# Attention and FFN kernel: the first FFN product of batches 3 to 6 with two block pairs as seven half products for eight

## The chip, the cores and the metric

The kernel runs on one core of a Trainium2 chip. The metric is device microseconds of one execution. The figure compared is the median over several runs.

## The reference

There are 8 batches, 8 heads of 64 columns, 512 local and 32 global positions. The local queries see the global keys and a band of 32 positions to each side; the global queries see everything. The result is the input of an FFN with a sigmoid gelu.

```python
s_g = scale * q_g @ concat(k_g, k_l).T          # global rows: no mask
out_g = softmax(s_g) @ concat(v_g, v_l)
s_ll = where(|i - j| <= 32, scale * q_l @ k_l.T, -1e9)
out_l = softmax(concat(scale * q_l @ k_g.T, s_ll)) @ concat(v_g, v_l)
x = concat(out_g, out_l) per batch, heads side by side   # 8 * 544 rows, 512 columns
h = x @ w_in                                     # 512 -> 2048, the first FFN product
out = (h * sigmoid(1.702 * h)) @ w_out           # 2048 -> 512, the second
```

## The kernel before

All work is laid out by hand: the order of the instructions in the program is the order on each engine's queue. Heads go in two groups of four, a `Quad` each: `a` is the first of a batch, `c` the second, `a2` the first of the batch after. The local rows of a batch are 512 tokens, held as `xL[i]` (model columns in four chunks of 128 on the partitions); the global rows of all batches gather in `xG` and are worked as a ninth batch at the end.

From batch 3 on the program alternates two stages.

**`h_some(i)`, the first FFN product of batch i.** The 2048 columns are 16 blocks of 128 (`fc`). A plain block (`h_step`) is four matmuls of 512 columns (line 617) into a PSUM bank `hp`, then a gelu on ScalarE (line 622) into `gT`. Blocks 2 and 3 are a block pair `g = 1`, worked by `HPair` in Winograd's form: seven products of half the columns and half the depth, two matmuls of 256 columns each (line 699), where eight would be needed. It takes weight sums made once, during batch 0 (`h_weight_sums`, line 660, kept in `early`), and sums of the input `xL` made on VectorE at the end of the stage before (`x_sums`, lines 673 and 674). The steps around the products are `m3` (copy on ScalarE), `z`, `zm`, `sub`, `add` on VectorE (lines 707, 710, 713, 716), and two gelus `inner` and `outer`. The pair's products lie in the two tiles of `spair()`, four PSUM banks. Batch 7 has a second `HPair` for `g = 4`. Between the blocks VectorE turns the keys and queries that the coming attention needs (`Tk`, `Tq`, lines 512 and 316), and `kcopy`, `qcopy` and `ext` copy parts of them and of the global keys and queries into place (lines 504, 507, 538 to 545). VectorE also makes `g_sums(i, lo, hi)`: four sums over block pairs lo to hi of `gT`, for the second product (lines 770 and 773). `k` is 0, 1, 2, 3, and the sum with `k = 2` is twice as long.

**`phase_o(i)`, the second product of batch i with the attention of batch i + 1.** The second product is Winograd too (`Pair`, line 800): `p0` and `p1` are two halves of the tokens, with `px` and `py` as banks. Between the products TensorE makes the scores (`S`, line 560) and the weighted values (`U` and `Gm`, together `UG`, lines 586 and 597). ScalarE takes the exponentials (`X`, line 571). `M` multiplies them with the band mask (line 576): on VectorE, but `a2.M(0)` on GpSimd. `R` makes the reciprocal of the row sums: a transpose `sT` (line 462), a reciprocal `rT` and a transpose back `rs`. `XL` multiplies the values with it into `xL`. `G` normalizes a quad's global rows and transposes them into `xG` (lines 476, 478, 479).

```python
exp_table()
a.UG()
c.S(0)
a.R()
g_sums(i, 7, 8, (0,))
a.XL(0)
g_sums(i, 7, 8, (1, 2))
a.XL(1)
g_sums(i, 7, 8, (3,))
p0.mm(3, 4, 1)
```

The matmul banks (`hp`, `ov`, `og`, `px`, `py`) rotate through four PSUM banks: `px` after `a.UG()` takes the bank of the first `ov`, which `R`'s `sT` frees, and `py` that of the second, which `XL(0)` frees. `loads_after` issues the loads of later batches from GpSimd's queue: nine for the values, one each for queries and keys.

Of the kernel before, what the change touches and what calls it, by code (L numbers as in the profile page):

```python
# [12 lines left out]
F32 = mybir.dt.float32  # L13
BF16 = mybir.dt.bfloat16
# [6 lines left out]
def kernel(  # L21
# [12 lines left out]
    nc = tc.nc  # L34

    B, H, Sl, D = q_l.shape
# [23 lines left out]
    att = ctx.enter_context(tc.tile_pool(name="att", bufs=2))  # L60
# [51 lines left out]
    def on_act(out_, in_):  # L112
        nc.scalar.activation(out_, in_, AF.Copy)  # L113
# [30 lines left out]
    early = ld.tile([128, 4, TB], F32, name="early", bufs=1)  # L144
# [131 lines left out]
    xG_by_row = xG.rearrange("p k (a s f) -> p k a s f", a=2, f=4)  # L276
# [3 lines left out]
    def pbank(name):  # L280
        return psP.tile([128, 512], F32, name=name, tag="p")
# [218 lines left out]
    class Wide(Quad):  # L500
# [100 lines left out]
        def UG(self):  # L601
            for unit in range(3):
                self.U(unit)
            self.Gm()

    gTs, ops = {}, {}
    HT = TB // 2
    HM = d_model // 2

    def width(i):  # L610
        return TB if i < B else B * Sg
# [23 lines left out]
    def exp_table():  # L635
        nc.scalar.activation(spot[:, 0:1], spot[:, 1:2], AF.Exp)

    def h_act(i, fc, hp):
        n = width(i)
        gelu(gTs[i][:, fc, :n], hp[:, :n])  # L640

    def h_step(i, fc):
        if fc == 0:
            gTs[i] = (moe.tile([128, FC, TB], BF16, name="gT") if i < B else
                      early.bitcast(BF16).rearrange("p a b -> p (a b)").rearrange("p (f t) -> p f t", f=FC))
        hp = pbank("hp")
        h_mm(i, fc, hp, range(NKC))
        h_act(i, fc, hp)

    w_h = {g: [w_in_c[:, g // 2, 2 * k : 2 * k + 2, g % 2, :, e] for e in range(2) for k in range(2)]  # L650
           for g in (1, 4)}
    w_s = early.bitcast(BF16).rearrange("p a b -> p (a b)")[:, : 5 * 2 * 256].rearrange(
        "p (k u c m) -> p k u c m", k=5, u=2, c=2)
    wh = {g: [w_s[:, k, u] for k in range(5)] for u, g in enumerate(w_h)}

    def h_weight_sums(g):
        w11, w12, w21, w22 = w_h[g]
        for t, x, y, op in zip(wh[g], (w11, w21, w11, w21, w12), (w22, w22, w12, w11, w22),
                               (ALU.add, ALU.add, ALU.add, ALU.subtract, ALU.subtract)):
            nc.vector.tensor_tensor(t, x, y, op)  # L660
# [93 lines left out]
    def g_sums(i, lo, hi, which=(0, 1, 2, 3)):  # L754
        n = width(i)
        if i not in sums:
            if i < B:
                sums[i] = [moe.tile([128, FC // 2, w * HT], BF16, name="gs%d" % k)
                           for k, w in enumerate((1, 1, 2, 1))]
            else:  # L760
                room = [ld.tile([128, 2, 16 * D], BF16, name=x).rearrange("p a b -> p (a b)")
                        for x in ("rk", "rq", "rk")]
                sums[i] = [x.rearrange("p (g t) -> p g t", g=FC // 2)
                           for x in (room[0][:, :1024], room[0][:, 1024:], room[1], room[2][:, :1024])]
        a11, a12, a21, a22 = parts_of(i)
        t = gTs[i].rearrange("p (g e) t -> p g e t", e=2)
        g = slice(lo, hi)
        for k in which:
            if k == 2:
                nc.vector.tensor_tensor(sums[i][2][:, g, :n], t[:, g, 0, :n], t[:, g, 1, :n], ALU.add)  # L770
            else:
                x, y, op = {0: (a11, a22, ALU.add), 1: (a21, a11, ALU.subtract), 3: (a12, a22, ALU.subtract)}[k]
                nc.vector.tensor_tensor(sums[i][k][:, g, : n // 2], x[:, g], y[:, g], op)  # L773
# [75 lines left out]
    a, c = Quad(0), Quad(1)  # L849
# [81 lines left out]
    for fc in range(4, FC):  # L931
        h_step(0, fc)
        if fc == 4:
            h_weight_sums(1)
        if fc == 12:
            h_weight_sums(4)

    def osteps(i, *sts):
# [4 lines left out]
    a, c = nq[1]  # L943
# [71 lines left out]
    a, c = nq[2]  # L1015
# [22 lines left out]
    def loads_after(i):  # L1038
        if i + 2 < B:
            load_v(i + 2)  # L1040
        if i == 1:
            load_g(8, NQ)
        if i + 3 < B:
            load(i + 3)
# [49 lines left out]
    def phase_o(i):  # L1094
        b = i + 1
        a, c = nq[b]
        a2, c2 = quads_of(b + 1)
        p0, p1 = Pair(i, 0), Pair(i, 1)
        exp_table()
        a.UG()  # L1100
        c.S(0)
# [7 lines that stand above are left out]
        c.X(0)  # L1109
        p0.m3()  # L1110
        p0.z()
        a.G()
        c.M(0)
        c.S(1)
        c.X(1)
        p0.mm(6)
        p0.zm()
        c.M(1)
        p0.mm(5, 2)
        p0.sub()  # L1120
        p0.evict()
        p0.mm(7)
        p0.add()
        p0.store()
        if a2:
            c.UG()
            c.R()
            a2.S(0)
            a2.X(0)
            a2.M(0, nc.gpsimd)  # L1130
            loads_after(i + 1)
        else:
            pt = spair()
            c.U(0, bank(pt, 0))
            c.U(1, bank(pt, 2))
            c.U(2, bank(pt, 3))
            c.Gm(bank(pt, 1))
            c.R()
        c.XL(0)
        if a2:  # L1140
            c.XL(1)
            c.G()
        p1.mm(3, 4)
        p1.m3()
        p1.z()
        if not a2:
            c.XL(1)
            c.G()
        p1.mm(1, 6)
        p1.zm()  # L1150
        x_sums(i + 1)
        if a2:
            a2.S(1)
            a2.X(1)
        p1.mm(5, 2)
        p1.sub()
        p1.evict()
        gelu_table()
        p1.mm(7)
        p1.add()  # L1160
        if a2:
            a2.M(1)
        p1.store()

    def h_some(i):
        c = nq[i + 1][1] if i + 1 < B else None
        a2 = quads_of(i + 2)[0] if i + 2 < B else None
        pool = nc.gpsimd.tensor_copy
        gTs[i] = moe.tile([128, FC, TB], BF16, name="gT")
        hps = [pbank("hp"), pbank("hp")]  # L1170
        for fc in range(2):
            h_mm(i, fc, hps[fc], range(NKC))
        p = HPair(i, 1)
        p.mm(3, 4)
        p.m3()
        for fc in range(2):
            h_act(i, fc, hps[fc])
        if c:
            c.Tk(False)
            c.kcopy(pool)  # L1180
        p.z()
        p.mm(1, 6)
        p.zm()
        if c:
            c.Tq(False)
            c.qcopy(pool)
            c.ext((3,), pool)
        if a2:
            a2.Tk(False)
            a2.kcopy(pool)  # L1190
        h_step(i, 4)
        if c:
            c.ext((0,), on_act)
        h_step(i, 5)
        p.mm(5, 2)
        p.sub()
        p.inner()
        p.mm(7)
        p.add()
        h_step(i, 6)  # L1200
        p.outer()
        if a2:
            a2.Tq(False)
            transpose_g(2 * i + 4, 2 * i + 6)
            a2.qcopy(pool)
            a2.ext(copy=pool)
        if c:
            g_sums(i, 0, 2)
        h_step(i, 7)
        if c:  # L1210
            c.ext((1,), on_act)
            g_sums(i, 2, 4)
            for fc in range(8, 12):
                h_step(i, fc)
                if fc == 9:
                    c.ext((2,), on_act)
            g_sums(i, 4, 6)
            h_step(i, 12)
            h_step(i, 13)
            g_sums(i, 6, 7)  # L1220
            h_step(i, 14)
            h_step(i, 15)
            return
        p = HPair(i, 4)
        p.mm(3, 4)
        p.m3()
        g_sums(i, 0, 2, (0, 1))
        p.z()
        p.mm(1, 6)
        p.zm()  # L1230
        g_sums(i, 0, 2, (2,))
        h_step(i, 10)
        h_step(i, 11)
        p.mm(5, 2)
        p.sub()
        p.inner()
        p.mm(7)
        p.add()
        g_sums(i, 0, 2, (3,))
        h_step(i, 12)  # L1240
        p.outer()
        for k in range(3):
            for lo in (2, 4):
                g_sums(i, lo, lo + 2, (k,))
        h_step(i, 13)
        h_step(i, 14)
        h_step(i, 15)
        g_sums(i, 6, 8, (0, 1, 2))
        g_sums(i, 2, 4, (3,))
        g_sums(i, 4, 6, (3,))  # L1250
        g_sums(i, 6, 8, (3,))

    for i in range(1, B):
        if i > 2:
            h_some(i)
        elif i > 1:
            for fc in range(FC):
# [3 lines left out]
                if i + 1 < B:  # L1261
                    c = nq[i + 1][1]
# [6 lines left out]
                    if fc == 9 and i + 2 < B:  # L1269
                        a2 = quads_of(i + 2)[0]  # L1270
# [19 lines left out]
    for st in range(FC):  # L1290
        h_step(B, st)
        if st < len(todo):
            tt, k = todo[st]
            if k == 3:
                p = Pair(B - 1, tt, pair_banks(tt))
# [19 lines left out]
    p = Pair(B, 0, (x0, x1, y0, y1))  # L1315
# [53 lines left out]
```

## Time and profile before

| what | value |
|---|---|
| median of 3 runs | 285.36 us (285.32 to 285.5) |
| profiled execution, its own time | 285.7 us |
| its span | 284.0 us |
| TensorE busy | 277.0 us (98%) |
| VectorE busy | 228.9 us (81%) |
| ScalarE busy | 182.1 us (64%) |
| GpSimd busy | 107.1 us (38%) |
| granted TensorE clock | 1.0 throughout |

The profile shows one execution. Its span runs from the first to the last instruction; the execution's own time is 1.7 us longer. In the timeline, an instruction's row gives its start, its length, and in brackets the idle time of its engine before it with what ended that. Successive rows of one engine can overlap by a tenth or two, because an instruction starts while the one before it drains; so the time from start to start is what a row of instructions costs, and the length is what one of them takes until others may use its result. "PE s L699" and "PE s L617" are matmuls into the tiles of `spair()`.

### The profile page before, as it was taken

Reading aid. Unit: us, or ns where it says so; the run is one execution under the profiler, and the core shown is the slowest. Engines: PE = TensorE matmul, PEld = TensorE weight load, DVE = VectorE, ACT = ScalarE, POOL = GpSimd, SP = SyncE. Lnnn points to the kernel's source line nnn. Section 1 sums busy time; section 2 is a strip of 40 time slices with the busy share of each in tenths; the row PEclk is TensorE's granted clock in tenths of the full one; section 3 lists DMA queues with packets and bytes.
Section 4 is the critical chain, followed back from the end, with each engine's and each line's share of the span. In section 5 each row is a group of like instructions: output and inputs, shape, how many; then the busy total and the mean of one; then the engine's idle time right before and its main releaser. Section 6 shows DMA issues by size and latency. Waiting matters only on the chain.

```text
span 284.0 us, 9001 instructions
## 1 busy us (share of the span) xinstructions
PE 277.0 (98%) x3763; PEld 182.3 (64%) x3763; DVE 228.9 (81%) x518; ACT 182.1 (64%) x299; POOL 107.1 (38%) x172
## 2 busy tenths in 40 slices
PE   7899999999999999999999999999999999999994
PEld 6454445544554488746885588647875589558884
DVE  7584458986689899999989998999988898586452
ACT  4858757577778784688457873788459761873331
POOL 8993550765946001990079302960041000000001
PEclk9999999999999999999999999999999999999999
DMA  7999995899999801795039802980022003200223
GB/s 208 159 195 210 203 162 77 148 217 144 170 165 183 151 2 48 78 177 91 14 69 163 150 5 68 84 97 3 21 58 74 2 3 76 74 3 0 58 54 112
DMA packets 59352, 28.24 MB, mean 99 GB/s; under 512 B 47472, under 2 KB 49776, under 8 KB 59312
## 3 DMA queue, kind: packets, MB, share of 16 engines
q0 software_dynamic: 51760, 17.83, 56.2%
q1 hardware_dynamic: 7120, 9.18, 11.7%
q8 instruction: 29, 0.48, 0.7%
q10 hardware_dynamic: 432, 0.66, 0.7%
q14 instruction: 11, 0.09, 0.1%
HBM read 36.31 MB, written 8.91 MB: 159 GB/s over the span
## 4 chain that ended last, share of the span: by engine, by line
PE 86%; DVE 7%; DMA 2%; issue 1%; POOL 1%; ACT 1%; DVEq 0%; POOLq 0%; ACTq 0%
PE hp L617 31%; PE px L800 12%; PE op L731 10%; PE py L800 9%; PE x L800 6%; PE s L560 5%; PE ov L586 5%; PE s L699 3%; PE s L617 3%; DMA rq<-in_q_l_dram 2%; DVE gs L773 2%; DVE gs L770 1%; DVE xL L471 1%; DVE kT L512 1%; PE og L597 1%
## 5 line engine op out<-in xcount | busy, mean ns | idle before, releaser
L617 PE MATMUL hp<-xL,w_in_sb 128*128 128x512 bf16 x432 | 97.0, 379 | 0.2 <-DVE xL L471 0.2
L617 PEld LDWEIGHTS <-w_in_sb 128*128 128x128 bf16 x528 | 51.4, 98 | 51.8 <-issue 0.4
L622 ACT ACTIVATE gT<-hp 128x512 bf16<-128x512 f32 x108 | 62.7, 600 | 17.1 <-PE hp L617 16.6
L571 ACT ACTIVATE e<-s 128x1016 bf16<-128x1016 f32 (+1 forms) x56 | 53.3, 1003 | 25.7 <-PE s L560 25.7
L800 PEld LDWEIGHTS <-gs 128*128 128x128 bf16 x480 | 46.2, 98 | 6.6
L576 POOL TENSOR_TENSOR e<-e,mask 128x1760 bf16<-128x1760 bf16 x4 | 13.3, 3320 | 70.0 <-ACT e L571 70.0
L98 POOL DMA_DIRECT2D v<-in_v_l_dram x40 | 31.1, 780 | 13.6 <-PE og L597 3.8
L773 DVE TENSOR_TENSOR gs<-gT 128x512 bf16<-128x512 bf16 (+1 forms) x87 | 31.6, 398 | 3.3 <-ACT gT L622 3.3
L800 PE MATMUL py<-wsum,gs 128*128 128x256 bf16 x240 | 30.3, 273 | 0.0
L731 PE MATMUL op<-w_out_sb,gT 128*128 128x512 bf16 x128 | 29.5, 380 | 0.0
L576 DVE TENSOR_TENSOR e<-e,mask 128x1712 bf16<-128x1712 bf16 (+1 forms) x24 | 25.2, 1049 | 3.5 <-ACT e L571 3.5
L512 DVE STREAM_TRANSPOSE kT<-rk 128x512 f32<-128x512 f32 x14 | 14.5, 1037 | 12.6 <-DMA rk<-in_k_l_dram 12.6
L833 POOL DMA_DIRECT2D out_dram<-ob x2 | 1.2, 596 | 60.5 <-ACT ob L113 60.3
L731 PEld LDWEIGHTS <-gT 128*128 128x128 bf16 x128 | 11.8, 98 | 14.0
L800 PEld LDWEIGHTS <-gT 128*128 128x128 bf16 x192 | 18.0, 98 | 3.0
L800 PE MATMUL px<-w_out_sb,gT 128*128 128x256 bf16 x160 | 19.2, 273 | 0.1
L800 PE MATMUL px<-w_out_sb,gs 128*128 128x256 bf16 x160 | 19.1, 273 | 0.0
L471 DVE TENSOR_TENSOR xL<-ov,rs 128x512 bf16<-128x512 f32 x27 | 17.9, 686 | 1.0 <-PE ov L438 0.3
L113 ACT ACTIVATE ob<-px 128x512 f32<-128x512 f32 x10 | 6.0, 599 | 19.3 <-DVE zz L822 19.3
L770 DVE TENSOR_TENSOR gs<-gT 128x1024 bf16<-128x1024 bf16 (+1 forms) x29 | 17.2, 598 | 0.0
L560 PEld LDWEIGHTS <-kT 32*128 32x128 bf16 x672 | 12.5, 93 | 6.8 <-issue 5.7
L100 POOL DMA_DIRECT2D v<-in_v_g_dram x24 | 14.0, 585 | 2.2 <-DMA rq<-in_q_l_dram 1.7
(176 smaller groups left out, 429.3 us busy)
## 6 DMA issues: line engine op xcount, KB each, us to landing
out_dram<-ob SPq DMA_DIRECT2D x128, 64.0 KB, 2.7
rq<-in_q_l_dram POOLq DMA_DIRECT2D x5, 512.0 KB, 8.2
rk<-in_k_l_dram POOLq DMA_DIRECT2D x5, 512.0 KB, 10.0
v<-in_v_l_dram POOLq DMA_DIRECT2D x24, 96.0 KB, 4.8
w_in_sb<-in_moe_w_in_dram POOLq DMA_DIRECT2D x8, 256.0 KB, 6.9
w_out_sb<-in_moe_w_out_dram POOLq DMA_DIRECT2D x4, 512.0 KB, 10.1
rk<-in_k_l_dram POOLq DMA_DIRECT2D x5, 256.0 KB, 7.8
rq<-in_q_l_dram POOLq DMA_DIRECT2D x5, 256.0 KB, 7.2
```

Of the source, the lines that this page charges most:

```text
L98: nc.gpsimd.dma_start(out=vt[0:n, hs, c, :D], in_=vs[FIRST[c] : FIRST[c] + n, hs])
L471: nc.vector.tensor_mul(self.x[:, 2 * self.u + h, :], self.st[1 + h], self.st["rs"])
L512: nc.vector.transpose(flat[:, 0:Sl].rearrange("p (r t) -> p t r", t=16), loaded[self.b][0][:, self.u].bitcast(F32))
L560: nc.tensor.matmul(bank(self.ps, j)[:, at : at + n], lhsT=self.k[p, KEYS[c] : KEYS[c] + 128, e], rhs=qs[p, :, :, e], start=(e == 0), stop= ...
L571: nc.scalar.activation(self.E[rnd][:, 2 * i : 2 * i + 2, :n], self.ps[i][:, :, :n], AF.Exp, scale=scale)
L576: eng.tensor_mul(e, e, mask[:, rnd : rnd + 1, :n].to_broadcast([128, 4, n]))
L617: nc.tensor.matmul(hp[:, : width(i)], lhsT=w_in_c[:, fc // 4, kc, fc % 4 // 2, :, fc % 2], rhs=(xL[i] if i < B else xG)[:, kc, :], start=( ...
L622: nc.scalar.activation(out_, in_, AF.Gelu_apprx_sigmoid)
L731: nc.tensor.matmul(op, lhsT=gTs[i][:, fc, tci * 128 : tci * 128 + 128], rhs=w_out_sb[:, fc, :], start=(first and fc == 4 * f4), stop=(fc = ...
L770: nc.vector.tensor_tensor(sums[i][2][:, g, :n], t[:, g, 0, :n], t[:, g, 1, :n], ALU.add)
L773: nc.vector.tensor_tensor(sums[i][k][:, g, : n // 2], x[:, g], y[:, g], op)
L800: nc.tensor.matmul(out_, lhsT=lv[:, g, tt * 128 : tt * 128 + 128], rhs=rv[:, g, :], start=(g == 0 and k in ((1, 3, 4, 6) if self.apart els ...
```

## The change

In `h_some` of batches 3 to 6 a second block pair, `g = 2` (blocks 4 and 5), joins `g = 1` in one `HPair`, so each of its steps works on twice the columns. A third group of weight sums is made for it in batch 0. Around it:

- `c.Tq` and `a2.Tk` move ahead of the pair's `z`, and c's copies with them; the loads move from `phase_o` to behind these copies.
- `g_sums` runs in three sets (pair 0, pairs 1 to 3, pairs 4 to 6) instead of four.
- The mask product of `a2` in round 0 moves from GpSimd to VectorE, behind `p1.z()`; that of round 1 moves from VectorE to GpSimd, at the end of `phase_o`.
- `a2`'s copies move from GpSimd in `h_some` to ScalarE in `phase_o` (for i over 2).
- `G` of the two quads becomes one `GG`, on a copy that ScalarE makes of each quad's PSUM result (`keep_og`).

```diff
+    def keep_og(q, ogs):
+        on_act(ogs[:, q.u], q.st["og"][:, : D + 2])
+
+    def GG(b, ogs):
+        rg = att.tile([128, 2, 1], F32, name="rgg")
+        nc.vector.reciprocal(rg, ogs[:, :, D : D + 1])
+        xg = att.tile([128, 2, D], BF16, name="xgg")
+        nc.vector.tensor_mul(xg, ogs[:, :, :D], rg.to_broadcast([128, 2, D]))
+        for u in range(2):
+            nc.vector.transpose(xG_by_row[:, 2 * u : 2 * u + 2, b // 4, :, b % 4],
+                                xg[:, u].rearrange("p (d h) -> p h d", h=2))
...
-           for g in (1, 4)}
+           for g in (1, 2, 4)}
...
         if fc == 12:
+            h_weight_sums(2)
             h_weight_sums(4)
...
 def phase_o(i):
+        ogs = att.tile([128, 2, D + 2], F32, name="ogs", bufs=1)
+        late = a2 and i > 2
...
         p0.z()
-        a.G()
+        keep_og(a, ogs)
+        if late:
+            a2.kcopy(on_act)
+            a2.qcopy(on_act)
         c.M(0)
         c.S(1)
         c.X(1)
         p0.mm(6)
         p0.zm()
         c.M(1)
+        if late:
+            a2.ext(copy=on_act)
         p0.mm(5, 2)
...
             c.UG()
             c.R()
+            keep_og(c, ogs)
             a2.S(0)
             a2.X(0)
-            a2.M(0, nc.gpsimd)
-            loads_after(i + 1)
...
         if a2:
             c.XL(1)
-            c.G()
+            GG(b, ogs)
         p1.mm(3, 4)
         p1.m3()
         p1.z()
-        if not a2:
+        if a2:
+            a2.M(0)
+        else:
             c.XL(1)
-            c.G()
+            GG(b, ogs)
...
         if a2:
-            a2.M(1)
+            a2.M(1, nc.gpsimd)
         p1.store()
...
 def h_some(i):
-        p = HPair(i, 1)
+        gs = (1, 2) if c else (1,)
+        fcs = iter([fc for fc in range(2, 8) if fc // 2 not in gs])
+        p = HPair(i, *gs)
         p.mm(3, 4)
         p.m3()
         for fc in range(2):
             h_act(i, fc, hps[fc])
         if c:
             c.Tk(False)
             c.kcopy(pool)
+            c.Tq(False)
+            c.qcopy(pool)
+            c.ext((3,), pool)
+            loads_after(i)
+        if a2:
+            a2.Tk(False)
         p.z()
         p.mm(1, 6)
         p.zm()
         if c:
-            c.Tq(False)
-            c.qcopy(pool)
-            c.ext((3,), pool)
-        if a2:
-            a2.Tk(False)
-            a2.kcopy(pool)
-        h_step(i, 4)
+            g_sums(i, 0, 1)
+        h_step(i, next(fcs))
         if c:
             c.ext((0,), on_act)
-        h_step(i, 5)
+        h_step(i, next(fcs))
         p.mm(5, 2)
         p.sub()
         p.inner()
         p.mm(7)
         p.add()
-        h_step(i, 6)
-        p.outer()
         if a2:
             a2.Tq(False)
             transpose_g(2 * i + 4, 2 * i + 6)
-            a2.qcopy(pool)
-            a2.ext(copy=pool)
-        if c:
-            g_sums(i, 0, 2)
-        h_step(i, 7)
-        if c:
+        if not c:
+            h_step(i, next(fcs))
+            p.outer()
+            h_step(i, next(fcs))
+        else:
+            h_step(i, 8)
+            p.outer()
+            g_sums(i, 1, 4)
+            h_step(i, 9)
             c.ext((1,), on_act)
-            g_sums(i, 2, 4)
-            for fc in range(8, 12):
-                h_step(i, fc)
-                if fc == 9:
-                    c.ext((2,), on_act)
-            g_sums(i, 4, 6)
+            h_step(i, 10)
+            c.ext((2,), on_act)
+            h_step(i, 11)
             h_step(i, 12)
             h_step(i, 13)
-            g_sums(i, 6, 7)
+            g_sums(i, 4, 7)
             h_step(i, 14)
             h_step(i, 15)
             return
```

More of the change, by code (lines that the diff above doesn't have):

```diff
@@ L650 @@
     w_h = {g: [w_in_c[:, g // 2, 2 * k : 2 * k + 2, g % 2, :, e] for e in range(2) for k in range(2)]
-           for g in (1, 4)}
-    w_s = early.bitcast(BF16).rearrange("p a b -> p (a b)")[:, : 5 * 2 * 256].rearrange(
-        "p (k u c m) -> p k u c m", k=5, u=2, c=2)
+           for g in (1, 2, 4)}
+    w_s = early.bitcast(BF16).rearrange("p a b -> p (a b)")[:, : 5 * 3 * 256].rearrange(
+        "p (k u c m) -> p k u c m", k=5, u=3, c=2)
     wh = {g: [w_s[:, k, u] for k in range(5)] for u, g in enumerate(w_h)}
@@ L1138, in phase_o @@
             c.R()
+            keep_og(c, ogs)
         c.XL(0)
```

## The prediction

> **What bounds the kernel now.** I read the page's chain that ended last first, then the same chain in order of time, then each engine's timeline around one batch. All times are microseconds of the profiled execution.
>
> ```profile
> PE 86%; DVE 7%; DMA 2%; issue 1%; POOL 1%; ACT 1%; DVEq 0%; POOLq 0%; ACTq 0%
> ```
>
> TensorE carries the end nearly alone. The chain in time shows what each piece costs it (start, length):
>
> ```profile
> 163.78 0.64 DVE sT L462
> 164.46 1.91 PE px L800 x16
> 166.37 0.96 PE py L800 x8
> ...
> 180.35 1.73 PE hp L617 x8
> 182.08 0.87 PE s L699 x8
> 182.95 1.73 PE hp L617 x8
> 184.68 0.66 PE s L699 x6
> 185.34 8.63 PE hp L617 x40
> 193.97 1.20 PE ov L586 x59
> ```
>
> The last six lines are the first FFN product of batch 5, from 180.35 to 193.97, without a gap: a 512-column matmul takes 1.73/8 = 0.216, a half product of 256 columns 0.87/8 = 0.109. The first three lines are the one place in batches 3 to 6 where VectorE led: px waited for R's first transpose (sT). The windows of two `phase_o` stages, cut where TensorE starts `a.UG()`, price that:
>
> ```profile
> 162.39:180.35 17.96, 17.82 (x393) 15.24 (x394) 16.71 (x38) 10.85 (x14) 4.78 (x4) 1.00 0.14 34
> 193.97:211.66 17.69, 17.69 (x393) 15.19 (x394) 16.16 (x36) 10.74 (x14) 3.32 (x1) 1.00 0.13 33
> ```
>
> Columns: stage, length, then busy time (and instructions) of PE, PEld, DVE, ACT, POOL. With sT starting 1.32 after the stage's start (163.71) the stage lost 0.28; where it started 0.70 after (194.67) or 1.09 after (132.14, stage of 17.67), nothing. VectorE is busy 16.2 of 17.7 here and 13.3 of 13.6 in the first product, so what it does last before sT decides. Its rows, and those of the engines it waits for:
>
> ```profile
> 143.99 3.32 POOL L576 TENSOR_TENSOR e<-e,mask 128x1760 bf16<-128x1760 bf16 x1 [16.21 <-ACT e L571]
> 145.86 2.07 DVE L673 TENSOR_TENSOR sT<-xL 128x512 bf16<-128x512 bf16 x2
> 239.86 0.73 DVE L673 TENSOR_TENSOR sT<-xL 128x512 bf16<-128x512 bf16 x2
> ...
> 191.18 0.68 DVE L770 TENSOR_TENSOR gs<-gT 128x1024 bf16<-128x1024 bf16 x1
> 191.78 1.08 DVE L773 TENSOR_TENSOR gs<-gT 128x512 bf16<-128x512 bf16 x3
> ...
> 246.48 0.69 DVE L713 TENSOR_TENSOR ob<-ob,s 128x512 f32<-128x512 f32 x1 [0.91 <-PE s L699]
> ...
> 21.10 1.94 ACT L622 ACTIVATE gT<-s 128x1024 bf16<-128x1024 f32 x2 [3.52 <-PE s L617]
> 192.28 0.60 ACT L622 ACTIVATE gT<-hp 128x512 bf16<-128x512 f32 x1 [0.27 <-PE hp L617]
> ```
>
> Two x-sums take 2.07 while GpSimd runs its mask product and 0.73 (batch 7) without it. The last row is the gelu of block 13: it waits only for TensorE and ends at 192.88, 1.09 before the stage.
>
> **The change on TensorE.** Per batch 3 to 6, eight matmuls of 0.216 (1.73) become fourteen of 0.109 (1.53): -0.20, four times **-0.80**. The 0.098 weight load of each half product stays under its 0.109. [...]
>
> **Edits that I cost at nothing, with their cover.**
> - Weight sums of the third group: five more of 0.34 start-to-start, 1.7, behind 24.85; VectorE then idles 7.34 until the keys land at 32.19.
> - Masks: the product moved to VectorE is 1.06, the one moved off 1.04. The x-sums lose the contention (2.07 to 0.73). GpSimd's 3.32 now starts when X(1) ends, 0.8 before the first product, and has 14 until `a.UG()`. Behind it stand c's three copies (about 1.2, done at 3.9 into the product, needed at 15) and then the loads (nine of v, and in two batches q and k, up to 8): issued some 5.5 later, needed 20 later at the least.
> - Global outputs: two G of 0.68 start-to-start become one GG, about 0.9 (reciprocal 0.20, product 0.35, two transposes 0.17 each). One G leaves `p0`, where VectorE next waits for X(1) anyway; the other end grows 0.2. GG waits for `keep_og(c)`, ready at 10.5 of the stage, asked for at 12.6.
> - ScalarE's copies: `keep_og` is bounded by its copies of 0.29 (72 elements) and 0.37 (256); I take 0.26 each. kcopy and qcopy, by the same rows 0.33 and 0.5, stand ahead of c's X(1); m3 starts at 3.85 of the stage, so they end by 5.0, and X(1) starts at 5.27 today. Were that gone, the mask product, sub, evict and c.UG would follow late one for one. The four of `ext` (0.9) lie between 7.05 and the evict at 8.87.
> - Moving c.Tq and a2.Tk ahead of z: after x-sums without contention and no mask product behind `p1.add`, VectorE reaches c.Tk at 0.64 into the product instead of 2.36, z at 3.1; mm(5, 2), which overwrites what z reads, comes at 5.20. Without this cover z would cost up to 1.6.
>
> **The edit that costs: the tail of the first product.** Count from its start, with the stage beginning at 1.73 + 0.87 + 0.87 + 1.73 + 0.87 + 0.44 + 6.91 = 13.41.
> - sub follows mm(5, 2), at 6.10. On 512 elements it takes 0.68, on 256 0.41, so about 1.21 on 1024: 7.31. add: 7.41 to 8.63.
> - ScalarE is in order: inner (1024 elements, 0.92 start-to-start) from 7.34, gelu 8 at 8.26 (0.48), outer at 8.74 (0.95, source in SBUF), then gelus 9 to 12 (0.48 each) and two `ext` copies (0.21, 0.16): gelu 13 runs 11.98 to 12.58. Today's ends 1.09 before the stage; this one 0.83 before.
> - Sums of block pairs 1 to 3 wait for outer (9.79) and end at 12.1. Sums of pairs 4 to 6 wait for gelu 13. Start-to-start a sum is 0.20 on 256 elements, 0.34 on 512, 0.60 on 1024; so 0.47 on 768 and 0.87 on 1536, and the set is 3 x 0.47 + 0.87 = 2.28. Today only the last pair's set (0.94) needs gelu 13; the set of pairs 4 and 5 (1.61) can go before it.
> - sT so starts at 12.61 + 2.28 = 14.89, 1.48 into the stage, in all four batches. Queued behind it on VectorE are rT, rs and the product that frees py's bank; px waits for sT, py for that product.
>
> Price: at 1.32 the stage lost 0.28. One for one, 1.48 loses 0.44; by the transpose alone (px free at 1.13 at the latest by py's start of 3.79) 0.35. I take 0.39, the middle: four times **+1.56**. Batch 4's present 0.28 is contained in that: **-0.28**.
>
> **Sum.** -0.80 - 0.28 + 1.56 = +0.48 on the profiled execution's own 285.7 (span 284.0, 1.7 around it): 286.2. That run lies 0.3 above the median of 285.36; on the median it is **285.8**, +0.17%. About 0.2% (0.57) is what a measurement of this kernel can tell from no change.
>
> **The rivals.**
> - *The tail stays covered (faster).* If gelu 13 and the sums end 0.35 earlier, sT starts by 1.13 and nothing waits: -0.80 - 0.28, 284.3; half covered, 284.8. For it: in batch 6 VectorE waits 0.56 before sT, and its load falls by the contention. Against it: the 2.28 behind gelu 13 depend on no earlier slack. 0.18.
> - *The tail is longer (slower).* sub and add cost like two of 512 each (0.77 start-to-start, so 1.54 instead of 1.31). outer then starts at about 9.2 and everything behind it is 0.46 later: 0.85 a batch, +3.4 - 1.08, 287.7. It decides as soon as the loss exceeds 0.42 a batch, so a fifth of it is enough for 286.0 to 286.4. 0.38.
> - *The exchanged mask collides.* GpSimd's product made the first x-sum wait to its end (147.26). [...] In the new order the last x-sum starts at about 16.1 of the stage and the GpSimd product 0.84 later. If the x-sums come 0.84 later, the last one waits until 2.6 into the product; sub, add, three transposes and z follow, z ends at 7.7 where 5.2 was due: at least 2.5 a batch, 295. 0.05.
> - That the half products are not made is excluded by the built order: TensorE has 24 more matmuls.
>
> **How the numbers follow.** The forecast, 284.8 to 285.9, has 0.39. Chances: faster 0.18, same 0.39, slower 0.43 (0.38 and 0.05). The likeliest case is the sum, 285.8. The range reaches down past the half-covered tail to 284.5 and up to 287.0, which is 0.67 lost a batch, some two thirds of the way to the longer tail's full price; outside lie the fully covered tail, the end of the longer one, and the collision.
>
> **What would show it.** Right: in batches 3 to 6 gelu 13 ends about 0.8 before `phase_o`, the four sums on 768 and 1536 elements run from there without a gap, sT starts about 1.5 into the stage, and px follows it at once; the first product is 13.4 and the stages 18.0 to 18.1. Two x-sums at 0.73 show the exchange as costed. Wrong: stages of 17.7 (covered), TensorE waiting at mm(5, 2) (z late), x-sums near 2 or more, or X(1) waiting behind qcopy.

## The result and the profile after

The changed kernel takes 287.82 us by the median of 6 runs (286.86 to 288.5), the kernel before 285.36 (285.3 to 285.61): the ratio of the runs is 1.0078, 95% interval 1.0061 to 1.0095 (the two medians alone would give 1.0086). It is slower. The forecast was 285.8 in a range of 284.5 to 287.0; the result lies above it. The profiled execution is the fastest of the six, 286.86, with a span of 285.1.

The chain that ended last now has ScalarE in it, which the kernel before hadn't beyond 1%:

```profile
PE 79%; ACT 9%; DVE 8%; DMA 1%; issue 1%; SPq 0%; DVEq 0%
```

In order of time (start, length), from the last half products of batch 3's first FFN product into `phase_o(3)`:

```profile
122.02 0.89 PE s L711 x8
122.93 1.23 DVE ob L725
124.19 2.94 ACT gT L634 x4
127.34 0.49 ACT gT L634
127.98 1.47 ACT gT L634 x3
129.47 1.03 DVE gs L785 x2
130.50 0.87 DVE gs L782
131.36 0.47 DVE gs L785
131.83 0.64 DVE sT L462
132.51 1.91 PE px L812 x16
134.42 0.96 PE py L812 x8
135.59 0.49 issue
136.07 0.53 PE s L560 x13
```

Down to px this is the forecast's tail, step by step: mm(5, 2), sub, the gelus up to block 13, the four sums of pairs 4 to 6, sT. The last two lines are not in the forecast: TensorE stands for 0.49 in the middle of `c.S(1)`, waiting for nothing that the profile shows. The view of the waits, TensorE's rows, gives both (total, times, longest):

```profile
PE px L812 <- DVE sT L462: 1.3, 4, 0.3
PE s L560 <- issue: 0.5, 1, 0.5
```

The stages of batches 4 and 5, cut where `a.UG()` starts and where the next first product starts, answer to those of before (17.96 and 17.69):

```profile
162.47:180.63 18.16, 17.82 (x393) 15.25 (x394) 16.96 (x35) 12.86 (x23) 0.65 (x1) 1.00 0.37 75
194.04:212.20 18.16, 17.83 (x393) 15.24 (x394) 16.96 (x35) 12.85 (x23) 0.66 (x1) 1.00 0.14 33
```

Both lose 0.47 against an undisturbed 17.69; TensorE's busy time is that of the stalled stage before (17.82), 0.13 above the undisturbed one's 17.69. Counted from the first matmul of one `a.UG()` to that of the next, batch 4's stage and first product take 31.57 and batch 3's 32.24. So the gap in `c.S(1)` costs 0.67 there, more than the 0.49 that stands as idle time. And the rows that the forecast rested on:

```profile
114.18 0.74 DVE L685 TENSOR_TENSOR sT<-xL 128x512 bf16<-128x512 bf16 x2
129.47 1.03 DVE L785 TENSOR_TENSOR gs<-gT 128x768 bf16<-128x768 bf16 x2 [0.43 <-ACT gT L634]
...
199.79 1.89 ACT L571 ACTIVATE e<-s 128x992 bf16<-128x992 f32 x2 [0.36 <-PE s L560]
```

Two x-sums take 0.74, as costed. VectorE waits for gelu 13 before the last sums. c's X(1) waits for TensorE's scores, not for the copies put ahead of it.

### The profile page after: what moved, and what is told of

Same layout as the page of the kernel before. It is cut to its first block, busy times and chain, and to the rows that moved or that the text cites. A ratio compares the mean times of both kernels' runs of the same rounds, so it can differ in the third digit from the quotient of the medians.

```text
span 285.1 us, 9001 instructions
## 1 busy us (share of the span) xinstructions
PE 275.1 (96%) x3764; PEld 184.7 (65%) x3787; DVE 227.3 (80%) x497; ACT 188.7 (66%) x319; POOL 99.1 (35%) x154
## 4 chain that ended last, share of the span: by engine, by line
PE 79%; ACT 9%; DVE 8%; DMA 1%; issue 1%; SPq 0%; DVEq 0%
PE hp L629 22%; PE px L812 13%; PE op L743 10%; PE py L812 9%; ACT gT L634 7%; PE x L812 6%; PE s L560 5%; PE s L711 5%; PE ov L586 3%; PE s L629 2%; DVE gs L785 2%; DVE ob L725 2%; DMA early<-in_q_l_dram 1%; DVE sT L462 1%; DVE gs L782 1%
## 5 line engine op out<-in xcount | busy, mean ns | idle before, releaser
L629 PE MATMUL hp<-xL,w_in_sb 128*128 128x512 bf16 x385 | 88.7, 379 | 1.0 <-DVE xL L471 0.2
L629 PEld LDWEIGHTS <-w_in_sb 128*128 128x128 bf16 x496 | 48.2, 98 | 48.1 <-issue 0.4
L634 ACT ACTIVATE gT<-hp 128x512 bf16<-128x512 f32 x100 | 57.6, 601 | 14.4 <-PE hp L629 13.7
L576 POOL TENSOR_TENSOR e<-e,mask 128x1712 bf16<-128x1712 bf16 x4 | 12.9, 3238 | 85.3 <-ACT e L571 85.3
L785 DVE TENSOR_TENSOR gs<-gT 128x256 bf16<-128x256 bf16 (+2 forms) x75 | 28.5, 406 | 5.9 <-ACT gT L634 5.9
L743 PE MATMUL op<-w_out_sb,gT 128*128 128x512 bf16 x122 | 28.8, 380 | 0.5 <-issue 0.3
L576 DVE TENSOR_TENSOR e<-e,mask 128x1760 bf16<-128x1760 bf16 (+1 forms) x24 | 25.3, 1052 | 4.3 <-ACT e L571 4.3
L560 PEld LDWEIGHTS <-kT 32*128 32x128 bf16 x672 | 12.5, 93 | 7.4 <-issue 5.5
L634 ACT ACTIVATE gT<-s 128x1024 bf16<-128x1024 f32 (+1 forms) x10 | 9.3, 938 | 11.8 <-DVE ob L725 7.3
L782 DVE TENSOR_TENSOR gs<-gT 128x512 bf16<-128x512 bf16 (+2 forms) x25 | 16.5, 664 | 0.0
L560 PE MATMUL s<-q,kT 32*128 32x160 bf16 (+1 forms) x448 | 14.7, 246 | 0.5 <-issue 0.5
```

What stands on the lines that cost most here:

```text
L560: nc.tensor.matmul(bank(self.ps, j)[:, at : at + n], lhsT=self.k[p, KEYS[c] : KEYS[c] + 128, e], rhs=qs[p, :, :, e], start=(e == 0), stop= ...
L576: eng.tensor_mul(e, e, mask[:, rnd : rnd + 1, :n].to_broadcast([128, 4, n]))
L629: nc.tensor.matmul(hp[:, : width(i)], lhsT=w_in_c[:, fc // 4, kc, fc % 4 // 2, :, fc % 2], rhs=(xL[i] if i < B else xG)[:, kc, :], start=( ...
L634: nc.scalar.activation(out_, in_, AF.Gelu_apprx_sigmoid)
L743: nc.tensor.matmul(op, lhsT=gTs[i][:, fc, tci * 128 : tci * 128 + 128], rhs=w_out_sb[:, fc, :], start=(first and fc == 4 * f4), stop=(fc = ...
```

## The experiments

Two theories fit this profile. **Tail:** the four sums behind gelu 13 make sT late, 0.47 a batch. **Transfer:** the queries and keys, now loaded some 10 us into the first product instead of 5, are still moving when `phase_o` begins, and the packets of the queue that the page marks "instruction" come late, so that TensorE stands for want of them: so far a guess. GpSimd's rows give the time of the issue, 5.3 into batch 3's first product in the kernel before and 10 into it in the changed one:

```profile
122.55 0.70 POOL L81 DMA_DIRECT2D rq<-in_q_l_dram  x1 [0.33 <-DVE q L316]
...
126.71 0.73 POOL L81 DMA_DIRECT2D rq<-in_q_l_dram  x1
```

Each comparison below is with the kernel before on the same chip.

### The changed kernel again

No edit.

> The changed kernel again, nothing edited. Both theories: a median near 287.8 us, with single runs between 286.8 and 288.5. In the profile sT (R's first transpose) starts 1.52 us after TensorE begins a.UG() in batches 3 to 6 and each of these four stages lasts 18.2 instead of 17.7. Tail theory alone: that is all, the remaining spread comes from the start of the program. Transfer theory (the loads issued 5.5 us later run into the stage in which TensorE takes most instructions, and its instruction supply waits): the profile shows gaps of TensorE ended by 'issue' of 0.3 to 1 us inside phase_o of batches 3 to 5, at other places or of other length than the 0.49 us of the first profile.

Measured: 287.09 us (287.01 to 287.31, 5 runs) against 285.52, ratio 1.0055 (1.0043 to 1.0067). The same four waits for sT of 0.34 at most, and the same gap, now longer:

```profile
PE px L812 <- DVE sT L462: 1.3, 4, 0.3
PE s L560 <- issue: 0.9, 1, 0.9
```

The gap sits at the same place, in `c.S(1)` of batch 3, and only there: of what the transfer theory expected, the other length came (0.9 for 0.5), the other places did not. By the rows it costs 1.06 here. The median lies 0.7 below the expected 287.8.

### The tail rearranged

```diff
         h_step(i, next(fcs))
+        if a2 and c:
+            a2.Tq(False)
         p.mm(5, 2)
         p.sub()
...
         if a2:
-            a2.Tq(False)
             transpose_g(2 * i + 4, 2 * i + 6)
...
             p.outer()
-            g_sums(i, 1, 4)
+            g_sums(i, 3, 4)
+            g_sums(i, 1, 3)
...
             h_step(i, 11)
+            g_sums(i, 4, 6)
             h_step(i, 12)
             h_step(i, 13)
-            g_sums(i, 4, 7)
+            g_sums(i, 6, 7)
```

> Changed kernel with the tail of the first product rearranged: a2.Tq moves ahead of sub (0.62 us into an idle 0.66), and g_sums runs as pair 3, pairs 1 to 2, pairs 4 to 5, pair 6 instead of pairs 1 to 3 and pairs 4 to 6. Tail theory: only the last set (0.94 us) waits for gelu 13, sT starts about 0.8 us into the stage, px waits for nothing, each of the four stages falls from 18.2 to 17.7, so 2.0 us less than the changed kernel on the same chip: near 285.8 by the median, 284.9 where nothing else disturbs. Transfer theory: the same 2.0 us less, but the runs keep a spread of more than 1 us. Rival (the lost time is not in the tail but in the half products or in ScalarE's copies): no change against the changed kernel.

Measured: 286.05 us (285.42 to 286.69, 12 runs), ratio 1.0018 (1.0009 to 1.0028); against the changed kernel -1.04, half of what was expected. In the profile no row has px waiting for sT any more, while `PE s L560 <- issue` is 0.9. The waits that the tail made are gone. In the two profiled executions each of the four stages is 0.47 to 0.49 shorter and the span 1.89, the tail's whole price. But they are the fastest of these twelve runs and the slowest of the changed kernel's five, and the medians differ by only 1.04. The twelve spread over 1.27 us, where those five spread over 0.30; what held up the slower ones isn't shown. The gap remains, so the tail alone isn't the whole loss.

### The loads earlier

```diff
             c.ext((3,), pool)
-            loads_after(i)
+            if i + 3 < B:
+                load(i + 3)
...
             a2.S(0)
             a2.X(0)
+            if i + 3 < B:
+                load_v(i + 3)
```

> Changed kernel with only the loads moved: the nine loads of the values are issued in phase_o behind a2.X(0), while GpSimd is idle, about 4 us earlier in the cycle than in the kernel before and 9 to 10 us earlier than in the changed one; the loads of queries and keys stay behind c's copies in h_some. Transfer theory: the TensorE gaps ended by 'issue' in phase_o go away, the runs lie within 0.5 us of each other and the median falls by 0.7 to 1.5 us against the changed kernel. Tail theory alone: stages of 18.2 us as before, the median and the spread of the changed kernel, within 0.3 us.

Measured: 286.41 us (286.23 to 287.85, 8 runs), ratio 1.0038 (1.0025 to 1.0052); -0.68 against the changed kernel, the lower end of what was expected. The profile shows no gap by 'issue' in `phase_o`, and the four waits of px for sT unchanged (1.3 in all). Seven of the eight runs lie within 0.6 us; the profiled one is the outlier, where TensorE waited 1.15 us at the first scores of batch 1 for a copy on ScalarE, which had itself waited 3.91 for a transpose on VectorE, long before anything that was edited; what held that up isn't shown.

### Both

The two edits above together.

> Both edits at once: the rearranged tail and the earlier loads. If both theories hold: stages of 17.7 us, no gap of TensorE in batches 3 to 6, 0.8 us for the half products and 0.3 us for the stall of batch 4 gained against the kernel before: 284.2 to 284.5 us, runs within 0.4 us. Tail theory alone: as the run with the rearranged tail only.

Measured: **284.65 us** (284.43 to 286.2, 12 runs) against 285.52, ratio 0.9975 (0.9964 to 0.9986): faster than both kernels. The queries go out 6 us earlier than in the changed kernel:

```profile
120.73 0.77 POOL L81 DMA_DIRECT2D rq<-in_q_l_dram  x1
```

The chain is TensorE's again:

```profile
PE 93%; DVE 2%; DMA 2%; ACT 1%; issue 1%; SPq 0%; DVEq 0%
```

From 53 us on TensorE has no gap of over 0.1. The absolute time is a little above the expected 284.2 to 284.5; the gain of 0.87 against the kernel before compares with 0.8 for the half products and 0.3 for the stall of batch 4. Some 0.3 of the missing part stands at the program's end: from TensorE's last product to the end of the span, every profile of the changed order has 3.9 to 4.0 us and both of the old order 3.6, for a reason that isn't shown. Between this run and the one with the loads alone lies the tail: 1.76, or 0.44 a batch. The two edits together are worth 2.44, each alone 1.04 and 0.68: the medians do not add up, and only the profiles' rows (0.47 a batch for the tail, 0.67 and 1.06 for the gap) price each by itself.

### The loads late in the kernel before

To see whether the late loads suffice without the change, in the kernel before:

```diff
             a2.M(0, nc.gpsimd)
-            loads_after(i + 1)
+            if i + 3 < B:
+                load_v(i + 3)
...
             a2.ext(copy=pool)
+        if i + 3 < B:
+            load(i + 3)
```

> The kernel before with one edit: the loads of queries and keys of batches 6 and 7 are issued in h_some behind a2's copies, some 10 us into the first product as in the changed kernel, instead of 5 us; the loads of the values stay. Transfer theory: in the stage that follows (batch 3, perhaps 4) TensorE waits 0.5 to 0.9 us for 'issue' inside c.S(1), and the median rises by 0.5 to 1.2 us, though the change itself isn't there. Rival (the gap comes from the changed order on TensorE or ScalarE): no gap, no change within 0.2 us.

Measured: 286.31 us (286.0 to 286.5, 5 runs) against 285.26, ratio 1.0033 (1.002 to 1.0046), +1.05. TensorE waits 0.8 for 'issue' in batch 3's `c.S(1)`. Stretches of 4 us from the end of batch 3's first product on, with the columns as above (the last but one is the DMA engines' share), kernel before:

```profile
129.00:133.00 4.00, 4.00 (x127) 2.58 (x126) 3.96 (x12) 3.17 (x6) 0.00 (x0) 1.00 0.59 110
133.00:137.00 4.00, 4.00 (x55) 3.29 (x56) 3.90 (x13) 2.94 (x5) 0.00 (x0) 1.00 0.02 4
```

the kernel before with late loads:

```profile
129.00:133.00 4.00, 4.00 (x127) 2.58 (x126) 3.93 (x12) 3.18 (x5) 0.13 (x1) 1.00 1.06 168
133.00:137.00 4.00, 3.20 (x46) 2.47 (x46) 3.93 (x12) 2.31 (x5) 0.00 (x0) 1.00 0.52 98
```

the changed kernel:

```profile
129.00:133.00 4.00, 3.75 (x127) 2.77 (x126) 3.50 (x8) 3.71 (x6) 0.00 (x0) 1.00 1.03 182
133.00:137.00 4.00, 3.51 (x51) 2.71 (x49) 3.94 (x9) 2.75 (x7) 0.00 (x0) 1.00 0.39 74
```

and the version with both edits:

```profile
129.00:133.00 4.00, 4.00 (x130) 2.81 (x128) 3.93 (x11) 3.71 (x7) 0.00 (x0) 1.00 0.02 4
133.00:137.00 4.00, 4.00 (x57) 3.34 (x55) 3.81 (x10) 3.73 (x8) 0.00 (x0) 1.00 0.01 4
```

Where the DMA share is still 1.06 and 1.03 in the first of these stretches, TensorE loses busy time in the second (3.20 and 3.51 of 4.00); at 0.59 and 0.02 it loses none. (The 3.75 of the changed kernel is its wait for sT.) The packets of the queue marked "instruction" fit: in batch 3's stage the first of them starts 3.6 to 3.9 us after the stage's start in the changed kernel and in this one, 1.5 in the kernel before, 1.2 in the version with both edits. It takes no longer than others (0.9 to 1.0 us, the others 0.9 to 1.8); it starts late.

### Queries and keys alone late

The version with both edits, the load of queries and keys held back:

```diff
-            if i + 3 < B:
-                load(i + 3)
...
             h_step(i, 9)
+            if i + 3 < B:
+                behind(gTs[i][0:1, 9, 0:2])
+                load(i + 3)
```

> The version with the rearranged tail and the earlier loads, but the loads of queries and keys held back until gelu 9 (by a GpSimd copy of two of its values), some 10 us into the first product; those of the values stay early. Transfer theory: the gap in c.S(1) of batch 3 is back with 0.5 to 1 us and the median rises by 0.7 to 1.4 us, to that of the run with the rearranged tail only. Rival (it was the nine loads of the values that had to go earlier): no gap and no change within 0.3 us.

Measured: 286.02 us (285.77 to 286.8, 7 runs) against 285.26, ratio 1.0027 (1.0016 to 1.0038), where the version without it had 0.9975: 0.52%, or 1.5 us, of which the rows of batch 3 show 1.1. The gap of 0.9 is back. So it was not the nine loads of the values.

### One batch's loads late

The same, for batch 6's queries and keys alone (loaded in batch 3's product, `if i == 3`) and for batch 7's alone (`if i == 4`).

> The version with the rearranged tail and the earlier loads, with only the queries and keys of batch 6 held back until gelu 9 of batch 3; those of batch 7 stay early. If the price of a late load is paid in the stage behind it alone: a gap of 0.8 to 0.9 us in c.S(1) of batch 3, and 0.8 to 1.4 us more in all, as much as with both held back.

> The mirror of it: only the queries and keys of batch 7 held back, in batch 4. If each late burst costs, a gap of 0.5 to 0.9 us in batch 4's stage and as much in all. If batch 4's stage is spared (none of the profiles so far has a gap there, though the burst runs into it too): no gap and no change within 0.3 us.

Measured: batch 6's alone 286.57 us (285.85 to 288.61, 9 runs), ratio 1.0052 (1.003 to 1.0074), with the gap of 0.9 in batch 3's stage; batch 7's alone 284.92 (284.66 to 285.69, 10 runs), ratio 0.9986 (0.9975 to 0.9997), with no gap. In the profiles all of the price is paid in batch 3's stage, 1.2 with batch 6's load late. The medians say 2.2 for it (0.77%), where 0.8 to 1.4 was expected; those runs spread over 2.8 us, and the profiled one is their fastest.

In batch 4's stage the instruction packet is as late (3.8 to 4.7 us in the kernels with late loads), and in the changed kernel the DMA share of its first 4 us is 1.07, yet TensorE has no gap by 'issue' there. The traces say why, in part by an estimate. In all six profiles with the gap TensorE stops behind its 1,880th or 1,881st weight load, which is 8 matmuls into `c.S(1)` in the changed kernel and 14 in the kernel before. It goes on 2.2 to 2.4 us after the start of the late packet (136.07 after 133.75 in the changed kernel). In the five without the gap it reaches that place 3.2 us or more after the packet's start (135.81 after 132.50 in the kernel before). So in these traces the stop goes with a count of instructions and not with a place in the program. Some 253 recorded instructions of TensorE go with one packet on average (7,078 from the first packet's start to the 29th's in the kernel before); counted on by four packets, TensorE would come to the first two packets of batch 4's stage 2.5 us or more after their start, in every profile: late enough for none of them to hold it up. This is an estimate from these counts.

### The exchange of the masks undone

From the version with both edits:

```diff
             a2.S(0)
             a2.X(0)
+            a2.M(0, nc.gpsimd)
             if i + 3 < B:
                 load_v(i + 3)
...
-        if a2:
-            a2.M(0)
-        else:
+        if not a2:
             c.XL(1)
             GG(b, ogs)
...
-            a2.M(1, nc.gpsimd)
+            a2.M(1)
```

> The version with the rearranged tail and the earlier loads, with the exchange of the mask products undone: round 0 of a2 on GpSimd behind its exponential, round 1 on VectorE at the end of phase_o, as in the kernel before. Cover theory: two x-sums take 2.07 us again and the mask product stands ahead of c.Tk, so VectorE reaches z 1.7 us later, TensorE waits about 0.3 us at mm(5, 2), sub starts 1.5 us later and sT some 1.2 us beyond its slack: 1.4 us a batch in batches 3 to 5, less in 6, about 4 us more in all. Rival (the two masks have the same length on VectorE, 1.06 and 1.04 us, so the exchange is worth nothing): within 0.5 us of the version it is made from.

Measured: 288.52 us (288.42 to 288.89, 4 runs) against 285.26, ratio 1.0115 (1.0099 to 1.013): 1.4% or 4.0 us more than the version that it is made from. VectorE's rows in batch 4 show why:

```profile
179.13 2.09 DVE L685 TENSOR_TENSOR sT<-xL 128x512 bf16<-128x512 bf16 x2
...
183.44 1.04 DVE L576 TENSOR_TENSOR e<-e,mask 128x1712 bf16<-128x1712 bf16 x1
...
186.76 0.67 DVE L719 TENSOR_TENSOR ob<-ob,s 128x512 f32<-128x512 f32 x1
...
189.71 1.18 DVE L725 TENSOR_TENSOR ob<-ob,s 128x1024 f32<-128x1024 f32 x1
```

The x-sums take 2.09, where the changed kernel's took 0.74; the mask product stands ahead of the transposes, and z and sub come late: z waited for by mm(5, 2) (0.2 a batch), and the late sub holds up inner and outer on ScalarE, whose gelus hold the banks (0.4 a batch). The first products of batches 3 to 5 last 14.7 instead of 13.5, counted from TensorE's first matmul; the two waits are 0.65 of these 1.2, and what the rest is isn't shown. The place of the loss differs from the one expected (more in the first product, less at sT); the size is the expected one. Exchanging two masks of the same length (1.04 and 1.05 us on VectorE) is worth 4.0 us here. In the kernel before, GpSimd's product ran from 143.99 to 147.31, and the x-sum begun at 145.86 took 1.73; in the changed one, with no product beside it, one took 0.41.

## Why the prediction was wrong

- **The half products:** right. Batch 4's first product took 13.62 (180.35 to 193.97 in the profile before) and takes 13.41 (180.63 to 194.04), 0.2 a batch.
- **The tail:** the mechanism is right, and the term was mis-sized. sT was put 1.48 into the stage; it starts at 131.75, 1.52 after 130.23, counted as the windows are cut (0.06 behind the first row of `a.UG()`). The price was taken as the middle of 0.35 and 0.44, 0.39; measured 0.47 in the stages, 0.44 by the medians of the two versions with earlier loads that differ in the tail alone (the pair with late loads gives 0.26 by its medians and 0.47 by its rows). Four times that is 0.2 to 0.3 us more than forecast. One for one from the stalled stage of before (0.28 at 1.32) would have given 0.48.
- **The loads:** this is the step that failed. They were costed at nothing, "issued some 5.5 later, needed 20 later at the least". That looked only at who needs the data. Nobody was late for the data; what else would come late while they moved at their new place was not asked. In place of nothing, the move cost 0.67 in the rows of batch 3 in the first profile and 1.06 in the second. Loading earlier gives 0.68 us back by the medians, with the tail mended 1.4; loading late in the kernel before costs 1.05.
- **The covers:** all that were costed at nothing for VectorE and ScalarE held: X(1), evict, z, GG. The run with the masks undone shows what z's cover was worth.
- **The rivals:** the longer tail didn't come, sub and add took 1.22 each. The collision of the mask with the x-sums didn't come either: the last x-sum of batch 3 starts at 115.17, the GpSimd product at 116.17. One sum of the rivals is off: a half-covered tail would by its own terms (0.39 less half of 0.35 a batch) give 285.1 and not 284.8.

The sum with the measured terms is -0.80 - 0.28 + 4 x 0.47 + 0.68 = +1.48, against +1.57 in the repeated measurement. That it comes so close is in part luck: the price of the gap differs from run to run, and the 0.3 at the program's end stands neither in the forecast nor in this sum. The first measurement's +2.46 had single runs up to 288.5, and only its fastest execution was profiled. What held up the others, some 0.9 of the median, isn't shown; a gap of other length at the same place is a guess.

## What to carry to other kernels

A step that moves loads has two questions: by when is the data needed, and what else is transferred in the time when it will now run. Here, with queries and keys still landing at the start of a stage of many short matmuls (DMA shares of 1.03 to 1.07 over some 4 us), some 0.7 to 1.2 us were lost in one batch and nothing by 'issue' in the other of the two that were tried; at a share of 0.59 nothing was lost. And a set of instructions that waits for one late result should hold only what needs that result: splitting four sums over three block pairs into two pairs and one (with one transpose moved ahead of `sub`) started sT 0.6 us earlier and was worth 1.8 us by the medians once the loads were early.

## What the runs showed of the hardware

In the rows, TensorE stood 0.5 to 0.9 us with nothing to wait for that the profile shows, in the stage of batch 3, in every kernel with the late load of batch 6 and in none without. In the changed kernel, 1 MB of queries and keys, issued at 126.71 and 127.41, was still landing when that stage began at 130.23. The packets of the queue marked "instruction" are 16,384 bytes, 29 in an execution for which the profile records 7,526 matmuls and weight loads of TensorE in the kernel before and 7,551 in the changed one. The one in question started 3.5 to 3.9 us into the stage instead of 0.9 to 1.6. TensorE stopped at the same count of weight loads, 1,880 or 1,881, in two different programs and went on 2.2 to 2.4 us after that packet's start. That TensorE stood for this packet is inferred from these counts and times in six traces. That the packet started late because the loads were moving is argued from these times; no run tested it by itself.
